# Three output-weight rows of each partition loaded apart by sixteen small transfers, and scores of two chunks summed at once

## The chip, the cores and the metric

The kernel runs on one NeuronCore of a Trainium2 chip. The metric is the device time of one execution in microseconds. Before the change three runs gave 525.9, 526.06 and 526.08 (median 526.06). Engines are named as in the profile: PE (matrix multiply), DVE (vector), ACT (scalar), POOL (GpSimd), SP (the queue that issues most transfers), and 16 DMA engines, which move the data.

## The reference

One decode step of a transformer block, four sequences, width 640:

```python
xn  = layernorm(x)
out = x + A(xn) + B(xn)
# A: attention, 32 heads of 192, the last W = 2048 of 8192 cached positions
q = xn @ wq
p = softmax(q . k[:, :, Sk-W:, :] * 192**-0.5)
A = (p @ v[:, :, Sk-W:, :]).reshape(B, 32*192) @ wo
# B: gated MLP of width 1536
B = (silu(xn @ w1) * (xn @ w3)) @ w2
```

All inputs and the output are bf16. Keys and values are 4 sequences x 32 heads x 2048 positions x 192, 100.7 MB each. Every byte of keys, values and weights is read once and used for four sequences (weights) or one (keys, values).

## The kernel before

**Tiles.** The 128 partitions are 32 heads x 4 (R) runs of positions. A load of keys or values (`load`, line 110) brings for one sequence b and one quarter s of the window 128 positions to each partition: 128 x 49152 bytes, 6144 KB. There are 16 of keys and 16 of values. Three buffers (`kv`) hold them; the first is used for `wq` before, and later ones for the MLP weights and for most of `wo`.

**Keys** (`keys`, four chunks c of 32 positions): DVE multiplies the chunk by q, which is laid out over all partitions in `qb` (`mult`, line 212). PE adds the 192 products of a position down to 16 by twelve matmuls with the identity into one PSUM bank (`adder`, line 219). DVE sums these 16 (`reduces`, line 229) into `sc`. A chunk's sum is issued after the multiply of the next chunk. **Values** (`chain`, `values`): maximum, exponential, then for each load a DVE multiply that spreads the weights over heads (`z`, line 268) and 64 matmuls (line 280). `evict`, `rowsum` and `sort` put the result of a sequence in `oT`, 128 partitions x 48 x 32: partition p holds rows 48p to 48p+47 of the 6144 that `wo` is multiplied with, the last dimension being the sequence (4 of 32 used).

**Order of work.** `units` begins with the four key loads of sequence 0 and then alternates: value load s of sequence b, key load s of sequence b+1. `stream` holds the loads from the third on, and then three groups: `gates` (w1, w3), `last_values` (the last value load in two halves, and ten rows of `wo` for each partition into a `pr` buffer) and `last_weights` (38 rows of `wo` in two loads of 26 and 12, then `w2` in three). The first two key loads are issued ahead of the loop. One entry of `stream` is issued before the loop and one after each unit, so that transfers are written down three units ahead of their use. A load also waits until its buffer is free.

**Queues.** Nearly all loads are issued on SP, which does them one by one: one that waits holds up what is behind it. The order on DVE and PE is pinned by hand (`ordered`, through `dve` and `pe`). On the other engines the framework picks the order: the one of the text, with ready instructions put ahead of others that are not. It also makes all semaphores. `x_load` (line 125) is called in the loop at b = 2, and the trace has its two transfers on POOL at 4.06 us, after POOL's last setup instruction.

**Start.** POOL clears `x_st`, builds the two identities `idb` and `idf`, and clears `scratch` and `oT`. DVE builds selection tiles and normalises x. PE transposes it (line 180), multiplies by `wq` (line 196) and lays q out over the partitions (line 205); ACT copies this into `qb` (line 206).

**End.** `ffn_mm`, `ffn_transpose` (MLP up to its hidden layer), the last values in two halves, `evict`, `sort`, then `proj` (line 315): for each of the 48 rows two matmuls into `acc`, first the ten rows of the `pr` buffer, then the 38. Then 24 matmuls with `w2` (line 423), one addition of both (line 426), and two stores: line 428 on SP, line 429 on ACT.

[...]

Of the kernel before, what the change touches and what calls it, by code (L numbers as in the profile page):

```python
# [10 lines left out]
FP32 = mybir.dt.float32  # L11
BF16 = mybir.dt.bfloat16
ALU = mybir.AluOpType
ACTF = mybir.ActivationFunctionType
AX = mybir.AxisListType
# [3 lines left out]
def kernel(  # L19
# [13 lines left out]
    CH: int = 32,  # L33
    R: int = 4,
    WI: int = 10,
    WM: int = 26,
    ALIGN: int = 64,
):


# [5 lines left out]
    nc = tc.nc  # L46
    P = 128
    B, Sq, D = A_x.shape
    _, H, Sk, Dh = A_k_cache.shape
# [3 lines left out]
    NJ = P  # L53
    NU = W // (NJ * R)
    NC = NJ // CH
    NK = Dh // DD
    SCALE = float(Dh) ** -0.5
    EPS = 1e-5
    NI = Dh // R
    NG = P // 32  # L60
    NH = H // NG
    QW = 2 * Dh
    NCH = 512
    DH = D // 2
# [11 lines left out]
    const = ctx.enter_context(tc.tile_pool(name="const", bufs=1))  # L76
    kvpool = ctx.enter_context(tc.tile_pool(name="kv", bufs=3))
    ppool = ctx.enter_context(tc.tile_pool(name="pr", bufs=2))
# [1 line left out]
    opool = ctx.enter_context(tc.tile_pool(name="o", bufs=1))  # L80
    small = ctx.enter_context(tc.tile_pool(name="small", bufs=2))
    ps_add = ctx.enter_context(tc.tile_pool(name="ps_add", bufs=2, space=MemoryType.PSUM))
    ps_o = ctx.enter_context(tc.tile_pool(name="ps_o", bufs=2, space=MemoryType.PSUM))
    ps_t = ctx.enter_context(tc.tile_pool(name="ps_t", bufs=3, space=MemoryType.PSUM))
    ps_acc = ctx.enter_context(tc.tile_pool(name="ps_acc", bufs=1, space=MemoryType.PSUM))

    ORDER_DEP = mybir.DependencyInfo(mybir.DependencyClass.NoSync, mybir.DependencyReason.SCHED_ONLY)
# [2 lines left out]
    def ordered(engine, inst):  # L90
        if engine in last:
            tc.add_manual_dep(inst.ins, last[engine].ins.name, ORDER_DEP, reason="issue order")
        last[engine] = inst
        return inst

    def dve(inst):
        return ordered("dve", inst)

    def pe(inst):
        return ordered("pe", inst)  # L100
# [3 lines left out]
    def load(which, b, s, n0=0, n1=NJ):  # L104
        if n0 == 0:
            kv = kvpool.tile([P, NJ, Dh], BF16, tag="kv")
            kvs[which, b, s] = kv
        p0 = Sk - W + s * NJ * R
        rows = {"k": A_k_cache, "v": A_v_cache}[which][b, :, p0:p0 + NJ * R, :].rearrange("h (r n) d -> h r n d", r=R)
        nc.sync.dma_start(out=kvs[which, b, s][:, n0:n1, :].rearrange("p n d -> p (n d)"),  # L110
                          in_=rows[:, :, n0:n1, :].rearrange("h r n d -> h r (n d)"))
# [8 lines left out]
    x_st = const.tile([64, DH], BF16, name="x_st")  # L120
    nc.gpsimd.memset(x_st[:], 0.0)

    def x_load():
        for t in range(2):
            nc.gpsimd.dma_start(out=x_st[32 * t:32 * t + B, :], in_=x_rows[:, t * DH:(t + 1) * DH])
# [7 lines left out]
    nc.sync.dma_start(out=wq1[:], in_=wq_rows[:, RV:KC, :])  # L133
    for s in range(2):
        load("k", 0, s)

    idb = const.tile([P, P], BF16, name="idb")
    make_identity(nc, idb[:])
# [16 lines left out]
    at = (NH - 1) * NG * R  # L155
    for b in range(B):
        nc.vector.tensor_copy(out=qwin[:, b, at:at + NG * R].rearrange("p (g r) -> p g r", r=R),
                              in_=idf[:, b:P:32].unsqueeze(2).to_broadcast([P, NG, R]))
    oT = const.tile([P, NI, 32], BF16, name="oT")
    nc.gpsimd.memset(oT[:], 0.0)  # L160

# [23 lines left out]
    acc = ps_acc.tile([64, DH], FP32, name="acc")  # L185

    q_pss = []
    for k in range(NH // 2):
        pool, tag = (ps_add, "ps") if k < 2 else (ps_o, "o_ps")
        qp = pool.tile([P, 512], FP32, tag=tag)  # L190
        q_pss.append(qp)
    for kc in range(KC):
        wq = (wq0[:, kc, :] if kc < RV else wq1[:, 0, :]).rearrange("p (k g d) -> p k g d", g=NG, d=Dh)
        for k in range(NH // 2):
            for g in range(NG):
                pe(nc.tensor.matmul(q_pss[k][32 * g:32 * g + 32, 0:QW], lhsT=xnT[:, kc, :], rhs=wq[:, 2 * k:2 * k + 2, g, :],  # L196
                                    start=(kc == 0), stop=(kc == KC - 1)))
# [10 lines left out]
    scs, es, rss, rcps, pend = {}, {}, {}, {}, []  # L208

    def mult(b, s, c):  # L210
# [2 lines left out]
                                    in1=qb[:, b, :].unsqueeze(1).to_broadcast([P, CH, Dh]), op=ALU.mult))  # L213
        return pr

    def adder(b, s, c, pr):
        ps = ps_add.tile([P, CH, DD], FP32, tag="ps")
        for kk in range(NK):
            pe(nc.tensor.matmul(ps[:], lhsT=idb[:], rhs=pr[:, :, kk * DD:(kk + 1) * DD], start=(kk == 0), stop=(kk == NK - 1)))  # L219
        pend.append((b, s, c, ps))  # L220

    def reduces():
        while pend:
            b, s, c, ps = pend.pop(0)
            if b not in scs:
                sc = small.tile([P, NU * NJ], FP32, tag="sc", bufs=1)
                scs[b] = sc
            at = s * NJ + c * CH
            dve(nc.vector.tensor_reduce(out=scs[b][:, at:at + CH], in_=ps[:], axis=AX.X, op=ALU.add))  # L229

    def keys(b, s):
        for c in range(NC):
            pr = mult(b, s, c)
            reduces()
            adder(b, s, c, pr)

    def chain(b):
        sc = scs[b]
        lmax = small.tile([P, 1], FP32, tag="lmax")
        dve(nc.vector.tensor_reduce(out=lmax[:], in_=sc[:], axis=AX.X, op=ALU.max))  # L240
        mt = ps_t.tile([P, P + 2], FP32, tag="t")
        pe(nc.tensor.transpose(out=mt[0:1, 0:P], in_=lmax[:], identity=idf[:]))  # L242
        gmax = small.tile([1, H], FP32, tag="gmax", bufs=1)
        dve(nc.vector.tensor_reduce(out=gmax[:], in_=mt[0:1, 0:P].rearrange("o (h r) -> o h r", r=R), axis=AX.X, op=ALU.max))  # L244
        gmq = small.tile([1, H, R], FP32, tag="gmq", bufs=1)
        dve(nc.vector.tensor_copy(out=gmq[:], in_=gmax[:].unsqueeze(2).to_broadcast([1, H, R])))  # L246
        pe(nc.tensor.matmul(mt[:, P:P + 1], lhsT=gmq[:].rearrange("o h r -> o (h r)"), rhs=nsc, start=True, stop=True))  # L247
        negm = small.tile([P, 1], FP32, tag="negm")
        dve(nc.vector.tensor_copy(out=negm[:], in_=mt[:, P:P + 1]))  # L249
        rs = small.tile([P, 1], FP32, tag="rs")  # L250
        e = small.tile([P, NU * NJ], BF16, tag="e", bufs=1)
        nc.scalar.activation(out=e[:], in_=sc[:], func=ACTF.Exp, bias=negm[:, 0:1], scale=SCALE, accum_out=rs[:])  # L252
        es[b], rss[b] = e, rs
# [48 lines left out]
    def wo_load(cuts, pool, tag, shape):  # L302
        wt = pool.tile(shape, BF16, tag=tag)
        flat = wt[:].rearrange("p a n -> p (a n)")
        for i0, i1 in zip(cuts, cuts[1:]):
            at = (i0 - cuts[0]) * D
            nc.sync.dma_start(out=flat[:, at:at + (i1 - i0) * D],
                              in_=A_wo.rearrange("(p i) n -> p i n", i=NI)[:, i0:i1, :].rearrange("p i n -> p (i n)"))
            for i in range(i0, i1):
                wos[i] = flat[:, at + (i - i0) * D:at + (i - i0 + 1) * D]  # L310

    def proj(i0, i1):
        for i in range(i0, i1):
            for t in range(2):
                pe(nc.tensor.matmul(acc[32 * t:32 * t + 32, :], lhsT=oT[:, i, :], rhs=wos[i][:, t * DH:(t + 1) * DH],  # L315
                                    start=(i == i0 and i0 == proj0), stop=(i == proj1)))
# [9 lines left out]
    def w2_load(i0, i1):  # L326
        if i0 == 0:
            ffn[2] = ffn["tile"][:, 2 * KC * F:2 * KC * F + NF * CF * D].rearrange("p (i n) -> p i n", n=D)
        nc.sync.dma_start(out=ffn[2][:, i0:i1, :], in_=B_w2.rearrange("(p i) n -> p i n", p=P)[:, i0:i1, :])
# [22 lines left out]
            pe(nc.tensor.transpose(out=hT_ps[:, c, :], in_=ffn["h"][0:32 * NF, c:NCH:CF], identity=idb[0:32 * NF, 0:32 * NF]))  # L352
        dve(nc.vector.tensor_copy(out=hT[:], in_=hT_ps[:]))

    proj0, proj1 = NI - WI, NI - WI - 1

    def last_values():
        for g in range(VS):
            load("v", B - 1, NU - 1, g * NJ // VS, (g + 1) * NJ // VS)
        wo_load((NI - WI, NI), ppool, "pr", [P, WI, D])  # L360

    def gates():
        ffn_load(1)
        ffn_load(3)

    def last_weights():
        wo_load((0, WM, NI - WI), kvpool, "kv", [P, NJ, Dh])
        for i0, i1 in ((0, (NF - 1) * CF), ((NF - 1) * CF, NF * CF - 1), (NF * CF - 1, NF * CF)):
            w2_load(i0, i1)

# [6 lines left out]
    def feed():  # L377
        fn, args = stream.pop(0)
        fn(*args)

    feed()
    for which, b, s in units[:-1]:
        if which == "k":
            keys(b, s)
        else:
            if s == 0:
                reduces()
                chain(b)
            values(b, s)
        if stream:  # L390
            feed()
        if which == "k" and b > 0:
            reduces()
            if s == 0:
                rowsum(b - 1)
                if b == B // 2:
                    x_load()
            elif s == NU - 1:
                sort(b - 1)
        if which == "v" and s == NU - 1 and b < B - 1:  # L400
            evict(b)
        if which == "v" and s == 0 and b == B - 1:
            rowsum(b)
# [4 lines left out]
        values(B - 1, NU - 1, g * NJ // VS, (g + 1) * NJ // VS)  # L408
    evict(B - 1)
    sort(B - 1)  # L410
    proj(NI - WI, NI)
    proj(0, NI - WI)

    t1 = opool.tile([64, DH], BF16, tag="t1")
    dve(nc.vector.tensor_copy(out=t1[:], in_=acc[:]))  # L415
# [4 lines left out]
    for i in range(NF * CF):  # L420
        n, c = i // CF, i % CF
        for t in range(2):
            pe(nc.tensor.matmul(ff[32 * t:32 * t + 32, :], lhsT=hT[:, c, 32 * n:32 * n + 32], rhs=ffn[2][:, i, t * DH:(t + 1) * DH],  # L423
               start=(i == 0), stop=(i == NF * CF - 1)))
# [34 lines left out]
```

## Time and profile before

| | |
|---|---|
| median of three runs | 526.06 us (525.9 to 526.08) |
| the profiled execution | 526.01 us |
| its span, first to last instruction | 524.1 us |
| mean granted TensorE clock | 0.873 |
| HBM read | 222.96 MB, 425 GB/s over the span |
| PE / DVE / ACT / POOL busy | 65% / 57% / 3% / 1% |

All times inside an execution are microseconds from the start of the span. In the profile, a group's line gives source line, engine, operation, `out<-in` by the program's names, partitions x elements, the count, and then busy time and the mean ns of one. "SPq" is a queue's own work: issuing a transfer, or waiting to issue it. A wait is put down to what came last before the waiting instruction went on. The chain of waits follows the execution back from its end, at each step to what released the instruction. Besides these views the trace keeps one record for each packet that a DMA engine moved, and the times at which the 16 engines marked their part of a load as complete.

### The profile page before, as it was taken

What the parts mean: (1) busy time and instruction counts of PE and PEld (TensorE: products, weight loads), DVE (VectorE), ACT (ScalarE), POOL (GpSimd) and SP (SyncE); (2) the same over time, 40 slices, a digit from 0 to 9 for tenths busy, and PEclk for the clock granted to TensorE, in tenths of its full rate; (3) what the DMA queues carried; (4) which work ended last, traced back from release to release, by engine and by line L of the source; (5) the groups of instructions that cost most, each with busy time, mean ns of one, the idle gap of its engine ahead of it and who ended that gap; (6) DMA issues with size and microseconds to landing.
All of it is one profiled execution on the core that took longest, in us unless ns stands there. A gap on an engine that the chain in (4) does not pass through costs nothing.

```text
span 524.1 us, 4690 instructions
## 1 busy us (share of the span) xinstructions
PE 341.9 (65%) x2147; PEld 199.4 (38%) x2147; DVE 300.5 (57%) x189; ACT 17.8 (3%) x34; POOL 4.7 (1%) x13
## 2 busy tenths in 40 slices
PE   0507677667676776596675866686565867688447
PEld 0302233253524352363434342353324353475445
DVE  4018999876583937676564828675574839411200
ACT  2110000000000000000000000000000000001100
POOL 3000000000000000000000000000000000000000
PEclk9977999979897887889798887998797888888797
DMA  9999999999999999999999999999999999999995
GB/s 361 431 448 439 420 425 447 439 421 424 436 450 425 420 435 451 431 418 439 443 433 424 424 455 431 425 420 450 436 431 421 435 448 428 428 420 427 432 425 240
DMA packets 6299, 223.26 MB, mean 426 GB/s; under 512 B 756, under 2 KB 904, under 8 KB 1032
## 3 DMA queue, kind: packets, MB, share of 16 engines
q1 hardware_dynamic: 6200, 222.96, 98.6%
q8 instruction: 16, 0.26, 0.2%
q14 instruction: 3, 0.02, 0.0%
q0 software_dynamic: 64, 0.01, 0.0%
q10 hardware_dynamic: 16, 0.01, 0.0%
HBM read 222.96 MB, written 0.01 MB: 425 GB/s over the span
## 4 chain that ended last, share of the span: by engine, by line
DMA 43%; DVE 29%; PE 25%; issue 1%; ACT 1%; SPq 0%; DVEq 0%; ACTq 0%
DMA kv<-in_A_k_cache_dram 38%; DVE pr L212 21%; PE o_ps L280 12%; PE ps L219 9%; DMA wt<-in_A_wo_dram 6%; DVE z L268 4%; DVE sc L229 4%; PE acc L315 2%; PE fp L296 1%; ACT e L252 1%; PE ft L423 0%; PE mt L247 0%; DVE gmax L244 0%; DVE gmq L246 0%; PE mt L242 0%
## 5 line engine op out<-in xcount | busy, mean ns | idle before, releaser
L212 DVE TENSOR_TENSOR pr<-kv,qb 128x6144 bf16<-128x6144 bf16 x64 | 213.4, 3351 | 104.7 <-DMA kv<-in_A_k_cache_dram 104.7
L219 PE MATMUL ps<-pr,idb 128*128 128x512 bf16 x768 | 194.1, 409 | 96.8 <-DVE pr L212 96.8
L219 PEld LDWEIGHTS <-idb 128*128 128x128 bf16 x768 | 79.5, 104 | 208.6 <-issue 122.6
L280 PE MATMUL o_ps<-kv,z 128*64 128x384 bf16 x1024 | 115.1, 396 | 50.6 <-DVE z L268 45.4
L280 PEld LDWEIGHTS <-z 128*64 128x64 bf16 x1024 | 94.5, 197 | 70.6 <-DVE z L268 53.0
L229 DVE TENSOR_REDUCE sc<-ps 128x32 f32<-128x512 f32 x64 | 43.9, 687 | 47.3 <-PE ps L219 47.2
L268 DVE TENSOR_TENSOR z<-e,selz 128x4096 bf16<-128x4096 bf16 (+1 forms) x17 | 36.7, 2158 | 18.2 <-PE o_ps L280 14.5
L315 PE MATMUL acc<-wt,oT 128*32 128x320 bf16 x96 | 9.5, 371 | 6.7 <-DMA wt<-in_A_wo_dram 6.1
L415 DVE CAST t<-acc 64x320 bf16<-64x320 f32 x1 | 0.5, 483 | 22.3 <-PE acc L315 22.3
L288 ACT COPY o_ev<-o_ps 128x384 f32<-128x384 f32 x4 | 1.9, 479 | 289.5 <-PE o_ps L280 289.5
L196 PE MATMUL qp<-wq,xnT 128*32 128x384 bf16 x80 | 5.2, 440 | 7.9 <-DMA wq<-in_A_wq_dram 7.9
L315 PEld LDWEIGHTS <-oT 128*32 128x32 bf16 x96 | 6.5, 118 | 9.5 <-issue 7.0
L296 PEld LDWEIGHTS fp<-o_ev,esel 128*128 128x128 f32 x64 | 7.7, 192 | 1.3 <-ACT o_ev L288 0.9
L296 PE MATMUL fp<-o_ev,esel 128*128 128x48 f32 x64 | 7.6, 272 | 0.6 <-ACT o_ev L288 0.6
L344 DVE TENSOR_TENSOR t_bf<-sg,t_bf 96x512 bf16<-96x512 bf16 x1 | 0.4, 420 | 11.5 <-ACT t_bf L338 11.5
L180 PE MATMUL xnT_ps<-idb,scratch 4*128 4x4 bf16 x5 | 0.4, 178 | 9.9 <-DVE scratch L176 9.9
L196 PEld LDWEIGHTS <-xnT 128*32 128x32 bf16 x80 | 3.1, 128 | 9.8 <-issue 7.5
L252 ACT ACTIVATE e<-sc,negm 128x512 bf16<-128x512 f32 x4 | 2.9, 721 | 80.5 <-DVE negm L249 80.5
L259 DVE RECIPROCAL rcp<-tb 128x1 f32<-128x1 f32 x4 | 0.6, 160 | 7.4 <-PE tb L257 7.4
L298 ACT ACTIVATE oT<-fp,rcp 128x48 bf16<-128x48 f32 x4 | 1.9, 468 | 64.9 <-PE fp L296 64.9
L180 PEld LDWEIGHTS <-scratch 4*128 4x128 bf16 x5 | 0.3, 125 | 9.9 <-DVE scratch L176 9.9
L205 PE MATMUL bp<-scratch 128*128 128x192 bf16 x32 | 3.3, 245 | 0.3
(60 smaller groups left out, 48.1 us busy)
## 6 DMA issues: line engine op xcount, KB each, us to landing
kv<-in_A_k_cache_dram SPq DMA_DIRECT2D x16, 6144.0 KB, 28.2
kv<-in_A_v_cache_dram SPq DMA_DIRECT2D x15, 6144.0 KB, 27.3
wq<-in_A_wq_dram SPq DMA_DIRECT2D x1, 6144.0 KB, 17.4
kv<-in_A_v_cache_dram SPq DMA_DIRECT2D x2, 3072.0 KB
wt<-in_A_wo_dram SPq DMA_DIRECT2D x1, 4160.0 KB, 29.4
ft<-in_B_w_dram SPq DMA_DIRECT2D x2, 1920.0 KB, 18.2
wt<-in_A_wo_dram SPq DMA_DIRECT2D x1, 1920.0 KB
wt<-in_A_wo_dram SPq DMA_DIRECT2D x1, 1600.0 KB, 27.8
```

Source lines behind the costliest of these rows:

```text
L196: pe(nc.tensor.matmul(q_pss[k][32 * g:32 * g + 32, 0:QW], lhsT=xnT[:, kc, :], rhs=wq[:, 2 * k:2 * k + 2, g, :], start=(kc == 0), stop=(kc ...
L205: pe(nc.tensor.matmul(bp[:], lhsT=qwin[:, b, w0:w0 + P], rhs=q_sb[:, k, :], start=(k == 0), stop=(k == NH - 1)))
L212: dve(nc.vector.tensor_tensor(out=pr[:], in0=kvs["k", b, s][:, c * CH:(c + 1) * CH, :], in1=qb[:, b, :].unsqueeze(1).to_broadcast([P, CH, ...
L219: pe(nc.tensor.matmul(ps[:], lhsT=idb[:], rhs=pr[:, :, kk * DD:(kk + 1) * DD], start=(kk == 0), stop=(kk == NK - 1)))
L229: dve(nc.vector.tensor_reduce(out=scs[b][:, at:at + CH], in_=ps[:], axis=AX.X, op=ALU.add))
L252: nc.scalar.activation(out=e[:], in_=sc[:], func=ACTF.Exp, bias=negm[:, 0:1], scale=SCALE, accum_out=rs[:])
L268: dve(nc.vector.tensor_tensor(out=z[:].rearrange("p h (a j) -> p h a j", j=ZB), in0=es[b][:, at:at + n].rearrange("p (a j) -> p a j", j=ZB ...
L280: pe(nc.tensor.matmul(o_pss[b][64 * t:64 * t + 64, 0:2 * Dh], lhsT=zf[:, a:a + (2 * H - 1) * half + 1:half], rhs=vt[:, n0 + a:n0 + a + hal ...
L288: nc.scalar.copy(out=o_ev[:].rearrange("p t d -> p (t d)"), in_=o_pss.pop(b)[:, 0:2 * Dh])
L296: pe(nc.tensor.matmul(fp[:], lhsT=esel[:, t, R - 1 - c:R - 1 - c + P], rhs=o_ev[:, t, c * NI:(c + 1) * NI], start=(c == 0 and t == 0), sto ...
L298: nc.scalar.mul(out=oT[:, :, b:b + 1].rearrange("p i o -> p (i o)"), in_=fp[:], mul=rcps.pop(b)[:, 0:1])
L315: pe(nc.tensor.matmul(acc[32 * t:32 * t + 32, :], lhsT=oT[:, i, :], rhs=wos[i][:, t * DH:(t + 1) * DH], start=(i == i0 and i0 == proj0), s ...
```

## The change

Of the 48 `wo` rows of each partition the last three (`WX`), 3840 bytes, no longer come with the others. They go to a tile of their own, `wx`, of two slots of three rows on every partition, which POOL first clears. Only half of the partitions are filled: with p = 64y + 32x + 16h + 4e + q, the partitions with h = y take the rows of both h = 0 (slot 0) and h = 1 (slot 1); the others stay zero. For each y there are eight transfers (x, q), each to four partitions (e), two pieces of 3840 bytes for each of these: 30.7 KB a transfer, 245.8 KB for each y. Those for y = 1 are issued on POOL in the setup, ahead of the identities; those for y = 0 stand on SP in the text of the loop, beside `x_load` at b = 2.

The load of 26 rows has 23 now; the ones of 12 and of ten rows are as large as before, but begin three rows earlier. `proj_ends` multiplies the three rows: two matmuls with a selection matrix `swap` bring the `oT` rows to the partitions that hold the weights, ACT copies them to `oX`, and twelve matmuls into `acc` follow, between the ten rows and the rest.

For the scores `ps_add` has tiles of two banks: chunks c and c+1 go to one tile, and one reduction sums both (1024 elements of each partition instead of 512). `ps_o` goes down to one buffer and `ps_t` to two. `ALIGN` changes the size of a padding tile.

```diff
-    WM: int = 26,
-    ALIGN: int = 64,
+    WM: int = 23,
+    WX: int = 3,
+    ALIGN: int = 192,
...
-    ps_o = ctx.enter_context(tc.tile_pool(name="ps_o", bufs=2, space=MemoryType.PSUM))
-    ps_t = ctx.enter_context(tc.tile_pool(name="ps_t", bufs=3, space=MemoryType.PSUM))
+    ps_o = ctx.enter_context(tc.tile_pool(name="ps_o", bufs=1, space=MemoryType.PSUM))
+    ps_t = ctx.enter_context(tc.tile_pool(name="ps_t", bufs=2, space=MemoryType.PSUM))
...
+    wx = const.tile([P, 2, WX * D], BF16, name="wx")
+    nc.gpsimd.memset(wx[:], 0.0)
+    wo_ends = A_wo.rearrange("(p i) n -> p i n", i=NI)[:, NI - WX:NI, :].rearrange("(y x h e q) i n -> y x q e h (i n)", y=2, x=2, h=2, e=4)
+    wx_rows = wx[:].rearrange("(y x h e q) h2 n -> y x h q e h2 n", y=2, x=2, h=2, e=4)
+    def wx_load(y, queue):
+        for x in range(2):
+            for q in range(4):
+                queue.dma_start(out=wx_rows[y, x, y, q], in_=wo_ends[y, x, q])
...
     for s in range(2):
         load("k", 0, s)
+    wx_load(1, nc.gpsimd)
...
+    swap = const.tile([P, 2, 4, 2, 16], BF16, name="swap")
+    for h in range(2):
+        nc.gpsimd.tensor_copy(out=swap[:, h], in_=idb[:].rearrange("p (a h r) -> p a h r", a=4, h=2)[:, :, h:h + 1, :].to_broadcast([P, 4, 2, 16]))
...
     def adder(b, s, c, pr):
-        ps = ps_add.tile([P, CH, DD], FP32, tag="ps")
+        if c % 2 == 0:
+            ps = ps_add.tile([P, 2, CH, DD], FP32, tag="ps")
+            adds[b, s] = ps
+        ps = adds[b, s]
         for kk in range(NK):
-            pe(nc.tensor.matmul(ps[:], lhsT=idb[:], rhs=pr[:, :, kk * DD:(kk + 1) * DD], start=(kk == 0), stop=(kk == NK - 1)))
-        pend.append((b, s, c, ps))
+            pe(nc.tensor.matmul(ps[:, c % 2], lhsT=idb[:], rhs=pr[:, :, kk * DD:(kk + 1) * DD], start=(kk == 0), stop=(kk == NK - 1)))
+        if c % 2 == 1:
+            pend.append((b, s, c - 1, ps))
...
-            dve(nc.vector.tensor_reduce(out=scs[b][:, at:at + CH], in_=ps[:], axis=AX.X, op=ALU.add))
+            dve(nc.vector.tensor_reduce(out=scs[b][:, at:at + 2 * CH], in_=ps[:].rearrange("p a j d -> p (a j) d"), axis=AX.X, op=ALU.add))
...
+    def proj_ends():
+        xp = ps_t.tile([P, 2, WX * 32], FP32, tag="t")
+        for o in range(2):
+            pe(nc.tensor.matmul(xp[:, o, :], lhsT=swap[:, o].rearrange("p a h r -> p (a h r)"),
+                                rhs=oT[:, NM:NI, :].rearrange("p i o -> p (i o)"), start=True, stop=True))
+        nc.scalar.copy(out=oX[:].rearrange("p o i b -> p (o i b)"), in_=xp[:].rearrange("p o n -> p (o n)"))
+        for o in range(2):
+            for i in range(WX):
+                for t in range(2):
+                    at = i * D + t * DH
+                    pe(nc.tensor.matmul(acc[32 * t:32 * t + 32, :], lhsT=oX[:, o, i, :], rhs=wx[:, o, at:at + DH],
+                                        start=False, stop=False))
...
                 if b == B // 2:
                     x_load()
+                    wx_load(0, nc.sync)
...
-    proj(NI - WI, NI)
-    proj(0, NI - WI)
+    proj(NM - WI, NM)
+    proj_ends()
+    proj(0, NM - WI)
```

More of the change, by code (lines that the diff above doesn't have):

```diff
@@ L187 @@
     q_pss = []
[L188 to L191, printed above, removed]
+    for k in range(0, NH // 2, 2):
+        qp = ps_add.tile([P, 2, 512], FP32, tag="ps")
+        q_pss += [qp[:, 0, :], qp[:, 1, :]]
     for kc in range(KC):
@@ L214, in mult @@
         return pr
+    adds = {}
     def adder(b, s, c, pr):
-        ps = ps_add.tile([P, CH, DD], FP32, tag="ps")
+        if c % 2 == 0:
+            ps = ps_add.tile([P, 2, CH, DD], FP32, tag="ps")
+            adds[b, s] = ps
+        ps = adds[b, s]
         for kk in range(NK):
-            pe(nc.tensor.matmul(ps[:], lhsT=idb[:], rhs=pr[:, :, kk * DD:(kk + 1) * DD], start=(kk == 0), stop=(kk == NK - 1)))
-        pend.append((b, s, c, ps))
+            pe(nc.tensor.matmul(ps[:, c % 2], lhsT=idb[:], rhs=pr[:, :, kk * DD:(kk + 1) * DD], start=(kk == 0), stop=(kk == NK - 1)))
+        if c % 2 == 1:
+            pend.append((b, s, c - 1, ps))
     def reduces():
@@ L353, in ffn_transpose @@
         dve(nc.vector.tensor_copy(out=hT[:], in_=hT_ps[:]))
-    proj0, proj1 = NI - WI, NI - WI - 1
+    NM = NI - WX
+    oX = const.tile([P, 2, WX, 32], BF16, name="oX")
+    def proj_ends():
[10 more added lines that the diff above has]
+                                        start=False, stop=False))
+    proj0, proj1 = NM - WI, NM - WI - 1
     def last_values():
@@ L359, in last_values @@
             load("v", B - 1, NU - 1, g * NJ // VS, (g + 1) * NJ // VS)
-        wo_load((NI - WI, NI), ppool, "pr", [P, WI, D])
+        wo_load((NM - WI, NM), ppool, "pr", [P, WI, D])
     def gates():
@@ L366, in last_weights @@
     def last_weights():
-        wo_load((0, WM, NI - WI), kvpool, "kv", [P, NJ, Dh])
+        wo_load((0, WM, NM - WI), kvpool, "kv", [P, NJ, Dh])
         for i0, i1 in ((0, (NF - 1) * CF), ((NF - 1) * CF, NF * CF - 1), (NF * CF - 1, NF * CF)):
```

## The prediction

> **What bounds the kernel now.** I read the page first, for the share of the transfers:
>
> ```profile
> DMA  9999999999999999999999999999999999999995
> ...
> q1 hardware_dynamic: 6200, 222.96, 98.6%
> ...
> DMA 43%; DVE 29%; PE 25%; issue 1%; ACT 1%; SPq 0%; DVEq 0%; ACTq 0%
> ```
>
> The queue that SP feeds keeps the 16 DMA engines 98.6% busy. The chain gives DVE 29% and PE 25%, but while they work the transfers run on all the same, so their durations are cover and not sum. Only three things can move the end: bytes on the engine that finishes last, a hole in the queue, and what follows the last landing. Busy time by stretch shows the last and the rate:
>
> ```profile
> 40.00:60.00 20.00, 14.98 (x58) 6.15 (x59) 18.24 (x10) 0.00 (x0) 0.00 (x0) 0.86 1.00 433
> ...
> 512.00:516.00 4.00, 4.00 (x34) 2.58 (x32) 0.00 (x0) 0.00 (x0) 0.00 (x0) 0.50 0.99 421
> 516.00:518.00 2.00, 2.00 (x26) 1.49 (x24) 0.00 (x0) 0.00 (x0) 0.00 (x0) 0.80 0.77 317
> 518.00:520.00 2.00, 2.00 (x34) 1.62 (x30) 0.53 (x2) 0.00 (x0) 0.00 (x0) 1.00 0.47 189
> 520.00:522.00 2.00, 1.03 (x16) 0.65 (x12) 0.76 (x2) 0.00 (x0) 0.00 (x0) 1.00 0.02 6
> ```
>
> The last columns are PE's clock, DMA share and GB/s. A full queue moves 433 GB/s, 27.1 per engine, so a 6144 KB load (6.29 MB) takes 14.5 us. From 516 on engines fall idle: the completion marks of the last load come at 516.9 to 517.8 on seven engines, 519.4 on one and 519.9 to 520.6 on eight. The eight late ones each carried two of the 16 packets of the instruction queue, about 1.5 us apiece. The chain in order of time shows what follows:
>
> ```profile
> 1.68 36.12 DMA kv<-in_A_k_cache_dram
> ...
> 482.04 29.37 DMA wt<-in_A_wo_dram
> 511.41 0.04 issue
> 511.45 7.95 PE acc L315 x76
> 519.40 1.64 PE ft L423 x24
> ```
>
> PE starts its last matmuls at 520.72 and the last weights land at 520.62: both bind. Then the order of SP:
>
> ```profile
> SPq L110 <- DVE pr L212: 230.4, 16, 16.6
> SPq L110 <- PE o_ps L280: 166.9, 13, 16.0
> SPq L428 <- DMA kv<-in_A_v_cache_dram: 13.4, 1, 13.4
> ```
>
> SP waits for buffers nearly all the time, and the queue stays full because it is one load ahead. The third line is the one that matters here. The store of line 428 reads only `res`, yet SP waited 13.4 us on a value load. That load (second half of the last values) stands eight transfers before the store, counting ACT's store in. I read it so: completion semaphores are reused in a rotation of eight, and a transfer is not issued until the one eight before it has landed.
>
> ```profile
> kv<-in_A_k_cache_dram SPq DMA_DIRECT2D x16, 6144.0 KB, 28.2
> ...
> wq<-in_A_wq_dram SPq DMA_DIRECT2D x1, 6144.0 KB, 17.4
> ```
>
> A load behind another lands 28.2 us after its issue (one load ahead); the first, into an empty queue, needs 17.4, that is 2.9 more than its 14.5.
>
> ```profile
> 1.14 0.12 DVE L182 MEMSET xnT<- 128x80 uint32 x1
> ...
> 1.98 0.29 DVE L145 TENSOR_REDUCE selh<-idf 128x32 f32<-128x128 f32 x1 [0.71 <-POOL idf masks.py:199]
> ...
> 2.73 1.37 POOL L160 MEMSET oT<- 128x1536 bf16 x1
> 4.06 1.19 POOL L125 DMA_DIRECT2D x_st<-in_A_x_dram  x2
> ...
> 27.00 0.32 ACT L206 CAST qb<-bp 128x192 bf16<-128x192 f32 x1 [0.34 <-PE bp L205]
> ...
> 37.92 6.63 DVE L212 TENSOR_TENSOR pr<-kv,qb 128x6144 bf16<-128x6144 bf16 x2 [27.43 <-DMA kv<-in_A_k_cache_dram]
> ```
>
> Line 182 ran before line 145: an instruction that is ready goes ahead of earlier ones that are not, on engines whose order is not pinned. SP's is not.
>
> **The change part by part.** The sum is made against the profiled execution, 526.01 us (span 524.1 and 1.9 around it); the median of three is 526.06, the same.
>
> *Eight transfers on SP (y = 0).* They need only the cleared `wx`, so once SP has issued the first two key loads (2.4 us) and the third must wait for its buffer, I expect them to go next, far ahead of their place in the text. Eight in a row fill the rotation, so the last must wait for the transfer just before the run: the second key load. It lands 14.5 after the first (37.8), at 52.3. Queued behind it in SP is the third key load, before issued at 22.8 with its data following without a hole. Now: wait to 52.3, issue of the eighth transfer and step to the next 0.6 (an issue takes 0.35 to 0.65), then 17.4 to land instead of 14.5. Slowest engine to slowest: 0.6 + 2.9 = +3.5. More is lost: by the completion marks of that load 15 engines are done at 49.9 to 50.8, one (the first to carry an instruction packet) at 52.3; the others now wait for it, +1.5, and the engines that finish last at the end are among them. So +5.0. Who waits: DVE needs the third key load at about 69.6 and gets it at 70.3, nothing; later loads are all issued on buffers, as before, one load ahead. If the eight keep their place in the text (behind the value load issued at 240.77, landing 269.7), the eighth waits for that load and the hole is the same +3.5; there the late engines themselves set the landing, so the 1.5 falls away. Their data, 61.4 KB on each of four engines, 2.3 us at 27.1, goes into the hole and costs nothing; without the hole it is +2.3 on those four.
>
> *Bounds of the hole.* Nearest row below: the store issued at 521.58 has its first packet 0.8 later, so 0.6 + 0.8 = +1.4 with no loss of order. Above: 3.5 + 1.5 and up to 2.3 more, where the POOL half has delayed four engines before the landing that is waited for. I take 5.0, and +0.4 for the POOL half: an early engine must first use up its lead of 1.5 to 2.3 before it is the one waited for.
>
> *Eight transfers on POOL (y = 1), clearing `wx`.* Clearing 3840 elements at 1.37 us per 1536 is 3.4; eight issues at 0.6 are 4.8. They stand before the identity in POOL, so identity, selection tiles and q come 8.2 later. `qb` is ready at 27.3 and the first multiply waits for keys until 37.92: 10.6 of cover, cost 0. Beyond it each us would be paid on DVE, then by the buffers.
>
> *Three rows out of the last weight load.* 491.5 KB less at 433 GB/s: −1.1 on every engine at the end.
>
> *PE at the end.* `proj_ends` is 14 matmuls at about 0.07 and an ACT copy near 0.5, some 2 us with the hops, in PE's idle 6.1 before line 315 (505.3 to 511.45): 0. The later part loses six matmuls, but ends on weights that land later: 0. If the landing came earlier, PE's half clock (0.50 in 512 to 516) would be next.
>
> *Scores of two chunks in one.* 64 reductions of 687 ns become 32; the row has no such shape. [...] DVE is ahead of the transfers after the first batch: 0. Fewer PSUM buffers for `o` and transposes: each user comes microseconds after the last is copied out, 0; uncovered, one copy of 0.5 each.
>
> Sum: +5.0 + 0.4 − 1.1 = +4.3 (in place: +3.5 + 0.4 − 1.1 = +2.8). 526.01 + 4.3 = **530.3 us**.
>
> **The rivals.** *No hole, better balance (faster, not slower).* If reuse of a semaphore does not hold SP, the late eight lose 1.1 while early engines fill up: 61.4 − 30.7 KB, +1.1 net. The last mark goes from 520.6 to about 519.8 (the engine at 519.4 holds it), PE follows: 525.3. For it: 3 us of idle engines at the end. Against: the store's 13.4. It decides if SP issues the third key load before 38.
>
> *No hole, but both halves on the same four engines.* POOL's two `x_st` loads of four partitions both went through the same four engines in the trace's packets. Then these get 2.3 more, and one with 519.4 ends near 522.2: 527.6. [...]
>
> *Each small transfer waits for the one before.* They write strided partitions of one tile; if these are taken as overlapping, eight follow one another in an empty queue at some 2 us (the store took 1.4 to land, and 0.5 to issue): +16 in place of the hole's +3.5, 542; POOL's eight, at 7.8 each (`x_st` issued 4.06, landed 11.8), would bring q late as well. Against: weights of lines 329 go into a tile while PE still reads other parts of it (issue 482.92, last read 484.6). [...]
>
> **How the numbers follow.** Hole at the start 0.55 (530.3; 528.5 to 532), hole in place 0.2 (528.8; 527.4 to 530.5), balance 0.1 (525.3), same four 0.09 (527.6), one by one 0.06 (540 and more). 527.4 to 532.2 leaves out the balance, the one by one and a little of each hole, 2 in 10. A change under 0.2% (1.05 us) can hardly be told from none: slower 0.86, same 0.1, faster 0.04 (the balance, if the refills of DVE's instructions fall out too).
>
> **What would show it.** A dip in the DMA digits at one place (50 to 55, or near 270); SP waits of the third key load's line or of the `wx` line on a key or value load, tens of us; DMA share under 98.6%; wt landing near 515.5; 32 reductions near 1.2 us. I am wrong if the DMA row stays at nines throughout, if SP issues the small transfers without a wait, or if the hole is under 1 us because the queue refills faster than at the start.

## The result, and the profile after

The changed kernel takes 531.73 us (median of four runs, 531.25 to 532.4) against 526.05 for the kernel before on the same chip: ratio 1.0109, 95% interval 1.0092 to 1.0127. The profiled execution took 531.28 with a span of 529.4, so the same 1.9 lie around the span as before and the two spans may be compared: +5.3.

From the page of the changed kernel (busy digits of the DMA engines, two queues, shares of the chain, the group of the reductions):

```profile
DMA  9999999999999999999979999999999999999996
...
q1 hardware_dynamic: 6296, 222.71, 98.0%
...
q0 software_dynamic: 320, 0.25, 0.2%
...
DMA 45%; DVE 29%; PE 22%; issue 3%; ACT 1%; SPq 0%; DVEq 0%; ACTq 0%
...
L249 DVE TENSOR_REDUCE sc<-ps 128x64 f32<-128x1024 f32 x32 | 39.0, 1219 | 36.9 <-PE ps L238 36.9
```

There is one 7 among the nines, in the slice of 265 to 278 us; the queue that SP feeds falls from 98.6% to 98.0%. In the chain DVE keeps its 29%, PE falls from 25% to 22%, and DMA and issue rise by 2 each. So the loss is in the transfers, and one place of it is near 270. What SP issued there (start, length from the first to the last of a group, line), first before and then after:

```profile
240.77 0.54 SPq L110 DMA_DIRECT2D kv<-in_A_v_cache_dram  x1
253.78 0.54 SPq L110 DMA_DIRECT2D kv<-in_A_k_cache_dram  x1
```

```profile
244.07 0.54 SPq L111 DMA_DIRECT2D kv<-in_A_v_cache_dram  x1
244.66 28.49 SPq L132 DMA_DIRECT2D wx<-in_A_wo_dram  x8
273.26 0.58 SPq L111 DMA_DIRECT2D kv<-in_A_k_cache_dram  x1
```

The eight transfers stand where the text has them, at b = 2. They take 28.5 us to issue, and the key load behind them leaves at 273.26. What SP waited for:

```profile
SPq L466 <- DMA kv<-in_A_v_cache_dram: 14.2, 1, 14.2
...
SPq L132 <- DMA kv<-in_A_v_cache_dram: 13.9, 1, 13.9
SPq L132 <- DMA kv<-in_A_k_cache_dram: 9.2, 1, 9.2
```

Six went at once. The seventh waited 9.2 for a key load and the eighth 13.9 for the value load issued at 244.07, neither of which it reads or overwrites; that value load landed at 272.52 and the eighth left at 272.53. In the trace the semaphores of SP's transfers go round in eights, and the eighth small transfer carries the number of that value load. Line 466 is the store at the end, with the wait that line 428 had before. POOL's queue shows the same: its second `x_st` load stands eight behind the second small transfer and waits 3.41 us for it, with no use for its data:

```profile
17.36 0.53 POOL L136 DMA_DIRECT2D x_st<-in_A_x_dram  x1 [3.41 <-DMA wx<-in_A_wo_dram]
```

What the wait on SP did to the transfers, by stretches (last two columns: DMA share, GB/s), first before and then after:

```profile
268.00:270.00 2.00, 2.00 (x10) 0.94 (x10) 2.00 (x2) 0.00 (x0) 0.00 (x0) 1.00 0.91 393
270.00:272.00 2.00, 0.88 (x5) 0.31 (x4) 2.00 (x2) 0.00 (x0) 0.00 (x0) 1.00 0.91 393
272.00:274.00 2.00, 2.00 (x11) 0.88 (x9) 0.39 (x1) 0.00 (x0) 0.00 (x0) 1.00 0.91 393
```

```profile
268.00:270.00 2.00, 1.14 (x6) 0.46 (x5) 2.00 (x2) 0.00 (x0) 0.00 (x0) 1.00 0.79 339
270.00:272.00 2.00, 2.00 (x11) 0.88 (x9) 2.00 (x2) 0.00 (x0) 0.00 (x0) 1.00 0.28 108
272.00:274.00 2.00, 0.35 (x2) 0.10 (x1) 1.78 (x1) 0.00 (x0) 0.00 (x0) 1.00 0.04 15
```

The engines ran dry for some 4 us; what moved at the end of the hole are the small transfers, each on four engines (followed end to start, the 56 packets of the first seven lie 14 each on four). And the end of the chain, in order of time:

```profile
487.87 36.54 DMA ft<-in_B_w_dram
...
524.46 1.95 PE ft L461 x24
```

PE starts its last 24 matmuls at 524.46 (before 519.40) and the last weights land at 526.03 (before 520.62): +5.41.

Where these 5.41 arise follows from the completion marks of four loads, slowest engine, in us of the span (read from the marks, before and after):

| load | before | after | later by |
|---|---|---|---|
| first keys | 37.79 | 40.65 | 2.86 |
| values ahead of the eight | 269.70 | 272.52 | 2.82 |
| keys behind the eight | 284.19 | 290.73 | 6.54 |
| last weights | 520.62 | 526.03 | 5.41 |

So +2.8 is there at the very start and stays, +3.7 comes at the hole, and −1.1 with the shorter last weight load. The first of these is not in the queue that SP feeds: by the packet records of 8 to 26 us, where POOL's eight transfers move, 50 of 107 packets of 49152 bytes (keys and most of `wq`) took over 1850 ns in place of 1815, up to 2161, and those of 12288 bytes (the rest of `wq`) a median of 605 in place of 460. Before, all 125 took 1815 there. The rate over those 18 us (last column), before:

```profile
8.00:26.00 18.00, 7.90 (x108) 5.32 (x109) 0.86 (x3) 3.37 (x8) 0.00 (x0) 1.00 1.00 429
```

and after:

```profile
8.00:26.00 18.00, 5.70 (x87) 3.54 (x88) 3.26 (x11) 1.33 (x4) 6.40 (x13) 1.00 1.02 393
```

### The profile page after: what moved, and what is told of

Read it like the earlier page. It is cut to its first block, busy times and chain, and to the rows that moved or that the text cites. A ratio compares the mean times of both kernels' runs of the same rounds, so it can differ in the third digit from the quotient of the medians.

```text
span 529.4 us, 4717 instructions
## 1 busy us (share of the span) xinstructions
PE 342.9 (65%) x2155; PEld 199.1 (38%) x2155; DVE 299.8 (57%) x157; ACT 18.2 (3%) x35; POOL 13.9 (3%) x24
## 4 chain that ended last, share of the span: by engine, by line
DMA 45%; DVE 29%; PE 22%; issue 3%; ACT 1%; SPq 0%; DVEq 0%; ACTq 0%
DMA kv<-in_A_k_cache_dram 38%; DVE pr L226 20%; PE o_ps L300 12%; PE ps L238 8%; DMA ft<-in_B_w_dram 7%; DVE z L288 4%; DVE sc L249 4%; ACT e L272 1%; DVE lmax L260 1%; PE ft L461 0%; PE mt L267 0%; PE mt L262 0%; DVE gmax L264 0%; DVE gmq L266 0%; SPq L327 0%
## 5 line engine op out<-in xcount | busy, mean ns | idle before, releaser
L300 PE MATMUL o_ps<-kv,z 128*64 128x384 bf16 x1024 | 118.0, 404 | 57.3 <-DVE z L288 50.2
L238 PEld LDWEIGHTS <-idb 128*128 128x128 bf16 x768 | 78.4, 103 | 203.1 <-issue 81.7
L300 PEld LDWEIGHTS <-z 128*64 128x64 bf16 x1024 | 95.9, 198 | 78.8 <-DVE z L288 57.5
L249 DVE TENSOR_REDUCE sc<-ps 128x64 f32<-128x1024 f32 x32 | 39.0, 1219 | 36.9 <-PE ps L238 36.9
L335 PE MATMUL acc<-wt,oT 128*32 128x320 bf16 x90 | 6.6, 299 | 3.7 <-DMA wt<-in_A_wo_dram 3.1
L195 PE MATMUL xnT_ps<-idb,scratch 4*128 4x4 bf16 x5 | 0.3, 171 | 10.5 <-POOL idb masks.py:199 10.5
L335 PEld LDWEIGHTS <-oT 128*32 128x32 bf16 x90 | 5.0, 96 | 5.2 <-issue 4.2
L132 POOL DMA_DIRECT2D wx<-in_A_wo_dram x8 | 5.3, 668 | 0.0
```

The source lines that it names most:

```text
L132: queue.dma_start(out=wx_rows[y, x, y, q], in_=wo_ends[y, x, q])
L238: pe(nc.tensor.matmul(ps[:, c % 2], lhsT=idb[:], rhs=pr[:, :, kk * DD:(kk + 1) * DD], start=(kk == 0), stop=(kk == NK - 1)))
L249: dve(nc.vector.tensor_reduce(out=scs[b][:, at:at + 2 * CH], in_=ps[:].rearrange("p a j d -> p (a j) d"), axis=AX.X, op=ALU.add))
L300: pe(nc.tensor.matmul(o_pss[b][64 * t:64 * t + 64, 0:2 * Dh], lhsT=zf[:, a:a + (2 * H - 1) * half + 1:half], rhs=vt[:, n0 + a:n0 + a + hal ...
```

## The experiments

Each ratio is to the kernel before, run on the same chip.

| run | what | us | ratio, 95% |
|---|---|---|---|
| the change | | 531.73 | 1.0109 [1.0092, 1.0127] |
| e1_six | six on SP, two behind the next load | 527.70 | 1.0028 [1.0016, 1.004] |
| e2_seven | seven and one | 531.87 | 1.0104 [1.0089, 1.0119] |
| e3_no_pool | POOL's half left out | 528.97 | 1.0051 [1.0036, 1.0066] |
| e4_pool_one | POOL's half as one, 64 partitions | 530.74 | 1.0096 [1.0074, 1.0119] |
| e5_pool_late | POOL's half after its setup | 531.12 | 1.0094 [1.008, 1.0107] |
| e6_six_no_pool | e1 and e3 together | 525.29 | 0.9983 [0.9974, 0.9992] |
| e7_pairs | before, with paired sums only | 526.01 | 0.9996 [0.9987, 1.0005] |
| e8_sp_one | as e4, but issued on SP | 530.79 | 1.0084 [1.007, 1.0098] |
| e9_six_far | e6, to other partitions | 529.28 | 1.0062 [1.0047, 1.0077] |
| e10_pool_128 | as e4, but 128 partitions | 529.19 | 1.0061 [1.0044, 1.0077] |
| e11_no_rows | the three rows not loaded | 524.90 | 0.9978 [0.9969, 0.9988] |
| e12_both_mended | e1 and e10 together | 525.95 | 1.0002 [0.9993, 1.0011] |

### Is it the count of eight? (e1_six, e2_seven)

```diff
-                    wx_load(0, nc.sync)
+                    wx_load(0, nc.sync, 0, 6)
...
+        if which == "v" and s == 1 and b == B // 2 - 1:
+            wx_load(0, nc.sync, 6, 8)
```

`wx_load` takes the numbers of the transfers that it issues; the second run has 7 for 6.

> The changed kernel with six of the eight small transfers on SP at their place, the other two behind the next key load. Hole theory: an SP transfer waits for the one eight before it in the common order; with six ahead of it, the key load that was issued at 273.3 waits only for the load before the last (landed at 258.0), so it is issued near 259 and no hole is left. The late engines then end with 2.4 us from POOL's half less 1.1, and the four engines of the small transfers carry 2.4 more: the last weights land near 523.2 instead of 526.0, time 528.0 to 529.2 (after: 531.3 to 532.4). Rival, that the 16 small transfers or their bytes cost the time and not the wait: 531 to 532, the same as the changed kernel.

> The same with seven ahead and one behind the next key load. Hole theory: the key load itself is now eighth behind the value load and must wait for its landing (272.5); it is issued 0.7 earlier than in the changed kernel, since one small transfer fewer is issued after that landing: 530.5 to 531.5, hole kept. Rival, that the cost goes with the number of small transfers in a row: a step of 1/8, some 0.5 us, between the changed kernel and e1 in proportion, so e1 would lose only 1 us.

SP's issues with six:

```profile
244.12 4.15 SPq L132 DMA_DIRECT2D wx<-in_A_wo_dram  x6
257.99 0.59 SPq L111 DMA_DIRECT2D kv<-in_A_k_cache_dram  x1
272.50 1.30 SPq L132 DMA_DIRECT2D wx<-in_A_wo_dram  x2
```

and with seven:

```profile
243.54 14.79 SPq L132 DMA_DIRECT2D wx<-in_A_wo_dram  x7
272.23 0.59 SPq L111 DMA_DIRECT2D kv<-in_A_k_cache_dram  x1
```

With six, the key load waits for the key load eight transfers before it and leaves at 257.99, a whole load ahead of need: no hole, and 4.0 us of the time are gone, a little more than expected (527.70 against 528.0 to 529.2). With seven the key load itself is the eighth behind the value load, leaves when that has landed, and the loss is whole. One transfer more or less decides, which no wait on the data or on a buffer would do. The 0.7 that seven was expected to save on eight (the eighth issue no longer stands ahead of the key load) does not show: the key load behind the run landed at 289.74 rather than 290.73, but 531.87 is no less than the changed kernel takes and 0.4 over the range given.

### What does POOL's half cost? (e3_no_pool, e5_pool_late, e6_six_no_pool)

```diff
-    wx_load(1, nc.gpsimd)
```

> The changed kernel without POOL's eight transfers (y = 1): their rows of wo are left out of the sum, 245.8 KB fewer are read. All 16 engines ended the first key load 2.4 us later in the changed kernel than before. If POOL's half does that: first key multiply at 37.9 to 38.3 instead of 40.75 and 528.4 to 529.3. If only its bytes count (0.57 us on each engine): first multiply at 40 and 530.7.

531.73 − 528.97 = 2.8 us for 245.8 KB, which at 433 GB/s are 0.57. It agrees with the +2.8 of the marks. For e5 the call stands behind `x_load()` in the loop instead:

> The changed kernel with POOL's eight transfers moved behind its setup work (beside the two x_st loads, some 10 us later), so that they are issued beside the first key loads and no longer beside the first weights of q. With the POOL half left out the time was 528.97, so the half costs some 2.8. Theory A (an engine loses the time wherever the POOL transfers run beside a full queue): 531.0 to 532.2, and the first key load lands as late as in the changed kernel or the second one does. Theory B (it costs only beside the first loads, while the queue starts): 528.8 to 529.6.

The first key load landed at 39.70, 0.95 earlier than in the changed kernel, but the value load ahead of the hole at 272.50, as late as there: the cost came later and was not much smaller (531.12, 2.2 over the run without the half). e6 takes both costs out:

> Six of SP's eight transfers in place and two behind the next key load (no hole), and the POOL half left out, so the rows of half of the partitions are not loaded and the output lacks them. Theory (hole and POOL half are the whole loss): the 526.05 of before less the 1.1 of three rows on the late engines, but the engine of the four that stood at 519.4 gets 2.3 more and ends near 520.7: 525.6 to 526.4. Rival (the paired reductions, the selection tiles or the smaller PSUM pools cost something as well): 527 or more.

525.29: faster than before by 0.17%, a little under what was expected, without the bytes of POOL's half. Beside these two, nothing in the change shows a cost. Hole and POOL half add up: 4.0 + 2.8 off 531.73 gives 524.9, within 0.4 of the run with both out. Between e3 and e6 the hole is worth 3.7, between e1 and e6 POOL's half 2.4.

### Queue, size or place? (e4_pool_one, e8_sp_one, e10_pool_128)

e4 sends the same 245.8 KB in one transfer, to the partitions they come from and not to those the selection expects; e8 sends the same one from SP, behind the first two key loads:

```diff
-    wx_load(1, nc.gpsimd)
+    nc.gpsimd.dma_start(out=wx[64:P, 0, :], in_=A_wo.rearrange("(p i) n -> p i n", i=NI)[64:P, NI - WX:NI, :].rearrange("p i n -> p (i n)"))
```

> The changed kernel with POOL's half as one transfer of 64 partitions x 3840 bytes into the upper half of wx, as many bytes; the upper rows then stand on other partitions than the multiplication takes them from, so the sum holds other terms. If the many small pieces slow all engines: first key multiply near 38.4, time 529 to 530. If it is POOL's bytes beside the first loads, whatever their form: the same as the changed kernel, 531.3 to 532.4, first multiply near 40.7.

> The changed kernel with POOL's half moved to SP, as one transfer of 64 partitions issued behind the first two key loads; the hole of SP's eight small transfers stays. The rows come to other partitions than the selection expects, so that the output is not the reference's. Theory A (the cost lies in POOL's way of issuing): 528.97 of the run without the half and 245.8 KB at 433 GB/s = 0.57 more, so 529.2 to 530.0. Theory B (it lies in the bytes or in their pattern on the memory's side): 530.6 to 532.

Both took 1.8 more than the run without the half, not 0.57; e4 fell between its two ranges, e8 into the one of theory B. So neither the number of transfers nor POOL's way of issuing makes these 1.8. In e8 the first key load was on time (37.42); the loss sat where the one transfer moved, at 49 to 54 us: all 30 packets of 49152 bytes beside it went over 1815 ns, up to 3049, and over half of its own 64 (36) over 149, up to 361. Left were the bytes' source (rows 61 KB apart) and their destination, 64 of 128 partitions. e10 keeps POOL, the place in the order, the byte count and the 61 KB step of the source, and takes 128 shorter pieces in place of 64:

```diff
+    nc.gpsimd.dma_start(out=wx[:, 0, 0:WX * D // 2], in_=A_wo.rearrange("(p i) n -> p (i n)", i=NI)[:, (NI - WX) * D:NI * D - WX * D // 2])
```

> The run with POOL's half as one transfer into 64 partitions (530.74), with the same 245.8 KB from POOL's queue at the same place spread over all 128 partitions, 1920 bytes each (half of the three rows of every partition, so the output is not the reference's). The hole of SP's eight transfers stays. Theory (partitions 64 to 127 alone are what 16 engines collide on): the time without the half, 528.97, and 0.57 for the bytes: 529.3 to 529.9, with the packets beside it at their 1815 ns. Rival (POOL's queue or the small packets cost it): 530.4 to 531.2, packets beside it slowed as before.

529.19, that is 0.2 over the run without the half (0.5 by the two ratios), about what the bytes alone are worth. The stretch of 8 to 26 us (last two columns DMA share and GB/s) in e4, then in e10:

```profile
8.00:26.00 18.00, 5.80 (x89) 3.59 (x90) 4.25 (x14) 3.40 (x7) 1.86 (x3) 1.00 1.00 399
```

```profile
8.00:26.00 18.00, 6.86 (x98) 4.33 (x99) 4.28 (x14) 4.09 (x9) 1.89 (x3) 1.00 1.03 443
```

The share is 1.0 in the changed kernel, in e4 and in e10; the rate is 393, 399 and 443. The share of busy time does not show this loss: the packets are on the engines, only longer. With 128 partitions none of the 125 large packets of that window took over 1820 ns.

The packet records also say where one transfer and eight differ. Sum what the packets that start before 60 us took beyond 1815 and 460 ns, add the whole time of the 245.8 KB, and divide by 16 engines: over the run without the half this is 2.4 us for the eight small transfers, 1.8 for e4, 1.8 for e8 and 0.6 for e10 (measured 2.8, 1.8, 1.8 and 0.2). Of the 2.4, 1.1 lies in the packets of 12288 bytes; in e4 not one of these is slow (at most 462 ns): they begin at 18.8, when POOL's packets have all moved (by 14.0). In the changed kernel POOL's packets move from 9.6 to 24.2, beside them.

So as many bytes cost more into 64 partitions than into 128 (1.8 us against 0.2), and the large packets beside them slow down as well (up to 3049 ns in e8, against 1820 at most in e10). Why they do, no run here shows.

### The same on SP's half (e9_six_far)

This is e6 with the destination changed, and with it the rows that belong there.

```diff
-                    wx_load(0, nc.sync, 0, 6)
+                    wx_load(1, nc.sync, 0, 6)
```

and the same for the last two.

> The run with six and two transfers on SP and no POOL half (525.29), with one thing changed: the eight transfers fetch the other half's rows and write them to partitions of 80 to 95 and 112 to 127 (y = 1) in place of those of 0 to 15 and 32 to 47. Bytes, queue, places in the order and sizes stay. The rows of y = 0 are left out. Theory (packets are slowed where an engine writes partitions that another engine serves in the large loads): the 64 packets of 3840 bytes take well over their 149 ns in part, packets of 49152 bytes beside them go over 1815 ns, and the time rises by 0.3 to 1.5: 525.6 to 526.8. Rival (the partitions do not matter; it is the number or the size of the packets that counts): packets at 149 and 1815 ns as before, 525.0 to 525.5.

By stretches, e6 and then e9 (last column GB/s):

```profile
266.00:268.00 2.00, 1.14 (x6) 0.45 (x5) 2.00 (x2) 0.00 (x0) 0.00 (x0) 1.00 1.00 424
268.00:270.00 2.00, 1.95 (x10) 0.78 (x8) 2.00 (x2) 0.00 (x0) 0.00 (x0) 1.00 0.99 424
270.00:272.00 2.00, 0.40 (x2) 0.19 (x2) 1.54 (x1) 0.00 (x0) 0.00 (x0) 1.00 0.92 399
```

```profile
266.00:268.00 2.00, 1.39 (x7) 0.58 (x6) 2.00 (x2) 0.00 (x0) 0.00 (x0) 1.00 1.28 334
268.00:270.00 2.00, 2.00 (x11) 0.88 (x9) 2.00 (x2) 0.00 (x0) 0.00 (x0) 1.00 0.59 142
270.00:272.00 2.00, 0.38 (x2) 0.10 (x1) 1.98 (x1) 0.00 (x0) 0.00 (x0) 1.00 0.98 308
```

+4.0 us for other partitions. The packets were as expected (37 of the 48 small ones of 266 to 280 over 149 ns, median 296; large ones up to 3492), the size was more than twice the upper end given. With the partitions 0 to 15 and 32 to 47 not one of the 64 small packets of e6 was slow. The rows read changed with the destination, in the same form and number; that they count for nothing is argued and not shown. Nor is the reason that the theory gives, which was my conjecture: the trace does not name the engine of a packet. A packet can only be followed from the one before it, since each begins within a few ns of the end of the one before it on its engine (2 to 4 ns at 150 to 200 us of the kernel before). Followed so, as far as the links can be told, the packets of POOL's eight transfers in the changed kernel lay on all sixteen engines, about two on each, and those of the first two transfers on eight different ones.

### What is left (e7_pairs, e11_no_rows, e12_both_mended)

e7 is the kernel before with the paired reductions (the hunks of `adder`, `reduces`, the q tiles and the PSUM pools of the change). e11 leaves both `wx_load` calls and `proj_ends` out. e12 is e1 with the POOL line of e10.

> The kernel before with only the scores of two chunks summed in one instruction and the PSUM pools that this needs; all 48 rows stay in the weight loads. Theory (DVE is ahead of the transfers): 525.8 to 526.4, the same time, with 32 reductions near 1.22 us. Rival (PE waits for the pair of banks, pr is freed later and the loads with it): 527 or more; other rival (DVE's 5 us reach the end): under 525.5.

> The changed kernel without both sets of eight transfers and without the matmuls that use them: the three rows are not loaded at all. The hole and POOL's half go; what is left of the change is the 491.5 KB less in the last weight load, the paired reductions and the clearing of wx. Theory (the last landing sets the end): 526.05 less 1.1, 524.6 to 525.3. Rival (PE's end sets it, at half clock): 525.4 or more.

> The changed kernel with both costs taken out: six and two transfers on SP (no hole), and POOL's half as one transfer over all 128 partitions (1920 bytes each, so the output is not the reference's). All bytes are moved. Theory (the two costs are the whole loss and add up): 525.29 of the run without the half, and 0.2 to 0.6 for its bytes: 525.5 to 526.0, which is before or barely under it. Rival (something is left that neither run showed): 526.5 or more.

e7 is the time of before. Its group of reductions:

```profile
L234 DVE TENSOR_REDUCE sc<-ps 128x64 f32<-128x1024 f32 x32 | 39.0, 1219 | 36.9 <-PE ps L223 36.9
```

5 us less on DVE (43.9 before), worth nothing. e11 at 524.90 is the −1.1 of the bytes alone. e12, with all bytes moved and both costs gone, is the time of before: 0.9993 to 1.0011. Its last marks show why: four engines end at 517.0 to 517.1, four at 518.9 to 519.4, seven up to 520.2 and one at 520.71 (before 520.62). The late engines lose 1.1 and get about 0.5 back with POOL's bytes, and one engine is last in place of them. I take it for one of SP's four, which get 2.3 more: in e11, without these bytes, no engine ended after 519.70. In e6, with SP's half alone, the last mark is 520.17. No run here that moved all the bytes beat the kernel before.

## Why the prediction was right or wrong

The direction, the range and the mechanism of the largest term held. The predicted 530.3 is 1.4 under the 531.73 measured, and that it came so close is luck: two errors cancelled in part, 1.5 too much for the place of the hole and 2.4 too little for POOL's half.

- **The hole: right.** A rotation of eight, read from one 13.4 us wait of the store, was the cause; e1 and e2 show it to the single transfer. Its size of 3.5 (0.6 + 2.9) measured 3.7 by the marks, and 3.2 to 4.0 by three pairs of runs with and without it (the change and e1, e3 and e6, e10 and e12).
- **Its place: wrong, and with it 1.5 of the sum.** That "once SP has issued the first two key loads" they would "go next, far ahead of their place in the text" did not happen. The framework puts ready instructions ahead on some engines, as line 182 on DVE showed, but no such row was of SP, and SP's eight were issued at 244.66 to 272.53, in the place of the text. The rival "in place" (chance 0.2) had the right place and left out the 1.5, rightly: at 270 the late engines set the landing (marks of 267.45 to 269.70 before). But its 528.8, with 530.5 at most, lay further from the time than the 530.3 did, for want of POOL's 2.4.
- **POOL's half: the mis-sized term.** It was put at +0.4, from bytes alone, against the lead of the early engines. It measured 2.8 (e3; marks 2.82 to 2.86), and not four engines but all sixteen ended the first key load some 2.4 later. The working counted bytes per engine and never asked which partitions the bytes go to, or whether the packets beside could grow longer. e4, e8 and e10 show 1.8 of it for 64 partitions (0.2 for 128); the rest goes with the packets of 12288 bytes that the eight transfers ran beside. The in-place sum with 2.8 in place of 0.4 is 526.01 + 3.5 + 2.8 − 1.1 = 531.2; the profiled execution took 531.28.
- **POOL's startup: right in the cost (0), wrong in the delay.** The clearing took 3.3 and the eight issues 5.3 (predicted 3.4 and 4.8), but q came only 2.3 later and not 8.2: its matmuls waited for the last of `wq` until 24.74, and the identity was there at 10.5. The first multiply waited for keys:

```profile
29.32 0.32 ACT L220 CAST qb<-bp 128x192 bf16<-128x192 f32 x1 [0.34 <-PE bp L219]
40.75 6.63 DVE L226 TENSOR_TENSOR pr<-kv,qb 128x6144 bf16<-128x6144 bf16 x2 [26.64 <-DMA kv<-in_A_k_cache_dram]
```

- **Three rows: right.** −1.1 by the marks and by e11.
- **Paired reductions: right.** 1219 ns each ("near 1.2"), cost 0 (e7). The 1.2 was an estimate: before had 687 ns for 512 elements and no reduction of 1024.
- **`proj_ends` and PE's end: right.** Its twelve matmuls with `wx` ran at 514.0 to 514.7, well before the last landing.
- **The rivals.** Balance fell with the 13.9 us wait. "One by one" fell, since six were issued within 4.2 us (e1). Their sums had slips: an engine that stands at 519.4 and gets 1.1 net ends at 520.5, not 519.8, so the balance comes to some 525.9, and the sum of "same four engines" rises by the same 0.7; e6 and e12, which have no hole, ended at 520.17 and 520.71. One by one comes to 541.3, not 542. "Same four engines" fell too: POOL's packets, followed end to start, lay on all engines. What I took from two `x_st` loads, which both lay on the same four, did not hold for these eight.

Two things stay open. The records carry no engine number: that the cost goes with the partitions written is inferred from e6 against e9 (525.29 and 529.28) and e4 against e10 (530.74 and 529.19), and why it does is not shown. And the packets' added time gives 2.4 of the 2.8 and, by the same sum, 2.8 of the 4.0 in e9; the rest is not accounted for.

## What to carry to other kernels

Count transfers, not only bytes: here completion semaphores were reused in a rotation of eight, and eight small transfers ahead of a big one turned a queue that was one load ahead into an empty one (15 GB/s at the low point, 3.2 to 4.0 us of the time), while six did not. The wait of a transfer on data that it didn't use, 13.4 us of the store, told the length of the rotation. And when bytes are moved apart from the others, choose their partitions too: here transfers of 30.7 KB into one set of partitions left packets as they were (149 and 1815 ns), and into another set lengthened their own (median 296) and the large ones (up to 3492). Only the GB/s and the packets' durations showed such a loss (399 GB/s in e4, 443 in e10), not the DMA share (1.0 in both).

## What the runs showed of the hardware that was not expected

- Eight transfers of 30.7 KB cost 4.0 us more into partitions 80 to 95 and 112 to 127 than into 0 to 15 and 32 to 47 (529.28 against 525.29), with packets of 49152 bytes stretched from 1815 to as much as 3492 ns.
- 245.8 KB into 64 partitions cost 1.8 us, from POOL or from SP; into 128 partitions 0.2.
- In the hole the rate fell to 15 GB/s in 272 to 274, and the refill was uneven: 17 of 80 large packets of 266 to 280 took over 1850 ns, up to 2641, in the changed kernel, against 1 of 121 in the run without a hole (e6).
